# Moving twenty half-tile sums from GpSimd to VectorE in a fused retention and feed-forward kernel

## The chip, the cores and the metric

The kernel runs on one core of a Trainium2 chip. The metric is the device time of one execution in microseconds (us). A core has five instruction queues that run side by side and meet only at semaphores: TensorE (PE in the profile; its weight loads are listed as PEld), VectorE (DVE), ScalarE (ACT), GpSimd (POOL) and SyncE (SP, which here issues nearly all DMAs). Each queue runs its instructions in the order in which they were written; an instruction that waits holds back all that stand behind it.

## The reference

Inputs are q, k and v of shape 8 x 8 x 576 x 64 (batch, head, position, head width) and two weight matrices. First comes a decayed linear attention, then a feed-forward layer whose activation is h cos(h):

```python
scores = scale * np.matmul(q, k.transpose(0, 1, 3, 2))
Dmat = np.where(rel >= 0, gamma[:, None, None] ** rel[None, :, :], 0.0)
attn = np.matmul(scores * Dmat[None], v)          # 8 x 8 x 576 x 64
x = attn.transpose(0, 2, 1, 3).reshape(4608, 512)
h = x @ w_in                                      # 4608 x 2048
out = (h * np.cos(h)) @ w_out                     # 4608 x 512
```

## The kernel before, in words

**Stages.** The 4608 tokens are worked on as nine tiles of 512 (numbered j = 0 to 8; TB, NTB). The attention runs in chunks of 64 tokens with a carried state and fills a ring of transposed inputs (XT). One attention step of two chunks (`step`) is a short group of small matmuls: the inter-chunk part (L617), the state update (L638), the intra-chunk part (L627) and the scores of the next step (L608). ScalarE and VectorE empty its banks.

**First product.** `mlp1` multiplies a tile with w_in. Four matmuls of 512 columns (L844) make one 128 x 512 piece in a PSUM bank; ScalarE takes its cosine (L852, a sine with a shifted phase, into one of three CB buffers), and VectorE multiplies the two (L855) into the tile G. There are sixteen pieces, f = 0 to 15, for each 512 tokens. Tiles alternate between two G buffers.

**Second product.** For tile 0 it is done directly (`mlp2`, L869). For tiles 1 to 8 it is a seven-product scheme on 2 x 2 blocks (`strassen` and `product`, L963). G is cut into two halves of the inner dimension (f = 0 to 7 and 8 to 15) and two halves of the tokens; w_out is cut likewise. Products m3 and m4 use blocks of G as they are. Products m2 and m5 need S5, the sum of the two halves of the inner dimension. Product m1 needs S1, the sum of the two diagonal blocks. Products m6 and m7 need differences, which are written over two blocks of G. Each product has two halves of 128 tokens (t = 0, 1), of eight matmuls of 256 columns each. S5 and S1 exist once, so the sums of a tile wait until the products of the tile before have read them.

**The sums.** `token_sums(j, u)` writes three VectorE or GpSimd instructions for a quarter u = 0 to 3 of tile j: S5 (L923, 128 x 1024), S1 (L928, 128 x 512) and the differences in place (L932, 128 x 1024). They read and write SBUF in bf16. In the profile's groups both S5 and S1 appear as `s`; the line and the width tell them apart. A quarter u needs pieces 2u, 2u+1, 2u+8 and 2u+9 of the tile, so the last quarter needs the last piece. The constant POOLED = 4 decides the engine of L928: for tiles 1 to 3 it is VectorE, for tiles 4 to 8 GpSimd. L923 and L932 are always on VectorE.

**Recombination.** ScalarE saves or copies finished banks (`save` L1002, `plain` L1007), VectorE and GpSimd add and subtract (`add`, L998): VectorE's steps read a bank, GpSimd's combine what lies in SBUF. For the last tile the products are asked for in the order m3, m4, m1, m2, m5, m7, m6, and m6 is emptied in two halves (`tail`), each with a store of its own.

**What sets the order.** All operations are added to a program with a cost, the buffers that they read and write, and two marks. `arrange` then plays through the program with these costs: every engine takes, in a small window of its list, the first operation that is ready, but an operation marked `lazy` only if no other is ready. Operations marked `port` queue for one shared lock between VectorE and GpSimd. The order that comes out is written down as each engine's queue, with semaphore waits. A changed cost or engine of one operation can so change the order on all engines after it.

Of the kernel before, what the change touches and what calls it, by code (L numbers as in the profile page):

```python
# [240 lines left out]


SOLO = 8
POOLED = 4
STB = 0


# [51 lines left out]
def ap(t, size, p0, n, off, *dims):  # L299
    return bass.AP(t, p0 * size + off, [[size, n]] + [list(d) for d in dims])  # L300


class Kernel:
# [610 lines left out]
    def token_sums(self, j, u):  # L914
        gt, f = self.GT[j % 2], 2 * u

        def half(k, t):
            return ap(gt, NF * TB, 0, 128, (f + HF * k) * TB + HB * t, [TB, 2], [1, HB])

        def keys(k, *ts):  # L920
            return [("gt", j % 2, f + HF * k + i, x) for i in range(2) for t in ts for x in range(4 * t, 4 * t + 4)]

        self.P.add("dve", lambda e: e.tensor_tensor(  # L923
            ap(self.S5, HF * TB, 0, 128, f * TB, [1, 2 * TB]), ap(gt, NF * TB, 0, 128, f * TB, [1, 2 * TB]),
            ap(gt, NF * TB, 0, 128, (f + HF) * TB, [1, 2 * TB]), ALU.add),
            r=keys(0, 0, 1) + keys(1, 0, 1), w=[("s5", f), ("s5", f + 1)], cost=0.62, port=True, lazy=True)
        eng = "pool" if j >= POOLED else "dve"
        self.P.add(eng, lambda e: e.tensor_tensor(  # L928
            ap(self.S1, HF * HB, 0, 128, f * HB, [HB, 2], [1, HB]), half(0, 0), half(1, 1), ALU.add),
            r=keys(0, 0) + keys(1, 1), w=[("s1", f), ("s1", f + 1)], cost=1.04 if eng == "pool" else 0.36,  # L930
            port=True, lazy=eng == "dve")
        self.P.add("dve", lambda e: e.tensor_tensor(  # L932
            ap(gt, NF * TB, 0, 128, f * TB + HB, [HF * TB - HB, 2], [TB, 2], [1, HB]),
            ap(gt, NF * TB, 0, 128, f * TB + HB, [HF * TB, 2], [TB, 2], [1, HB]),
            ap(gt, NF * TB, 0, 128, f * TB, [HF * TB, 2], [TB, 2], [1, HB]), ALU.subtract),
            r=keys(0, 0, 1) + keys(1, 0, 1), w=keys(0, 1) + keys(1, 0), cost=0.62, port=True, lazy=True)
# [299 lines left out]
```

## Time and profile before

| | us |
|---|---|
| median of 6 runs (299.27 to 300.22) | 299.62 |
| the profiled execution | 299.28 |
| its span, first to last instruction | 297.6 |
| PE busy | 289.4 (97%) |
| DVE busy | 231.4 (78%) |
| ACT busy | 186.8 (63%) |
| POOL busy | 174.0 (58%) |
| L928 on POOL, 20 instructions | 28.3 |
| L928 on DVE, 12 instructions | 8.2 |

The span is what the profile shows; the 1.7 us between it and the execution's own time lie around it. A line of a group reads: source line, engine, operation, output and inputs by the program's names, shapes, count, then busy time and the mean duration of one in ns, then the idle time of the engine just before them with the instruction that ended it. A line of the timeline reads: start and duration in us, engine, line, operation, count, and in brackets the idle time before it. Neighbouring instructions of one kind are merged. The matmul rows are pipelined and overlap a little, so their starts are the better guide. The granted TensorE clock is 1.00 in every stretch of the profile but the last (0.99).

### The profile page before, as it was taken

How to read it: one execution, taken by the hardware profiler on the slowest of the kernel's cores; microseconds unless marked ns; L12 is line 12 of the kernel's file. 1: busy time of each engine (PE TensorE's matmuls, PEld its weight loads, DVE VectorE, ACT ScalarE, POOL GpSimd, SP SyncE). 2: the span in 40 equal slices, each digit the busy share in tenths (PEclk: the TensorE clock that was granted, in tenths of full speed). 3: DMA queues.
4: the chain of work that ended last, by engine and by line, in shares of the span. 5: the costliest groups of instructions: out<-in, count | busy, mean ns of one | idle time of the engine just before them, and what ended most of it. 6: DMA issues, size and time to landing. Idle time of an engine off the chain costs nothing.

```text
span 297.6 us, 8942 instructions
## 1 busy us (share of the span) xinstructions
PE 289.4 (97%) x3751; PEld 204.1 (69%) x3751; DVE 231.4 (78%) x369; ACT 186.8 (63%) x317; POOL 174.0 (58%) x166
## 2 busy tenths in 40 slices
PE   8998899999999999999999999999999999999996
PEld 2567568765788885777566766676677576666685
DVE  6785899999789389779957995899489738964961
ACT  6256767826588276676667667766776777555511
POOL 4566650979856487287508992899274017402923
PEclk9999999999999999999999999999999999999999
DMA  7999999999999999999789898998211011102024
GB/s 204 303 328 325 287 180 221 201 233 230 228 255 160 174 282 197 214 193 196 166 182 261 177 176 212 212 155 185 58 35 57 19 40 40 47 21 70 2 70 141
DMA packets 123895, 50.12 MB, mean 168 GB/s; under 512 B 82384, under 2 KB 123344, under 8 KB 123856
## 3 DMA queue, kind: packets, MB, share of 16 engines
q1 hardware_dynamic: 121744, 47.46, 72.5%
q0 software_dynamic: 2112, 2.10, 4.4%
q8 instruction: 29, 0.48, 0.7%
q14 instruction: 10, 0.08, 0.1%
HBM read 36.70 MB, written 9.44 MB: 155 GB/s over the span
## 4 chain that ended last, share of the span: by engine, by line
PE 84%; DVE 5%; SPq 4%; DMA 3%; ACT 2%; issue 1%; DVEq 0%
PE bk L844 38%; PE bk L963 32%; PE bk L869 5%; DMA gt<-in_moe_w_in_dram 3%; PE st L638 2%; SPq L433 2%; PE bk L617 2%; DVE gt L855 2%; SPq L466 1%; PE bk L608 1%; PE bk L627 1%; PE bk L565 1%; SPq L452 1%; DVE s L923 1%; PE bk L552 1%
## 5 line engine op out<-in xcount | busy, mean ns | idle before, releaser
L844 PE MATMUL bk<-xt,win 128*128 128x512 bf16 (+1 forms) x744 | 138.9, 331 | 2.7 <-DVE gt L855 0.7
L852 ACT ACTIVATE cb<-bk,cpi 128x512 bf16<-128x512 f32 x144 | 98.3, 688 | 54.8 <-PE bk L844 51.0
L855 DVE TENSOR_TENSOR gt<-bk,cb 128x512 bf16<-128x512 f32 x144 | 96.2, 684 | 42.2 <-ACT cb L852 37.0
L844 PEld LDWEIGHTS bk<-xt,win 128*128 128x128 bf16 x744 | 70.8, 98 | 43.6 <-DVE pt L712 1.1
L532 POOL TENSOR_TENSOR qnat<-qstg,wt 128x512 bf16<-128x512 f32 x34 | 40.9, 1221 | 20.6 <-DMA qstg<-in_q_dram 20.6
L998 POOL TENSOR_TENSOR sv<-sv,os 128x512 f32<-128x512 f32 x16 | 20.4, 1274 | 48.4 <-ACT os L1007 35.5
L680 ACT ACTIVATE sbd<-st 64x512 bf16<-64x512 f32 x58 | 34.3, 592 | 11.7 <-PE bk L608 10.4
L494 POOL CAST nat<-stg 128x512 bf16<-128x512 f32 x32 | 25.1, 791 | 20.0 <-DMA stg<-in_k_dram 15.5
L928 POOL TENSOR_TENSOR s<-gt 128x512 bf16<-128x512 bf16 x20 | 28.3, 1423 | 13.4 <-DVE gt L855 13.4
L932 DVE TENSOR_TENSOR gt<-gt 128x1024 bf16<-128x1024 bf16 x32 | 34.1, 1070 | 0.2
L522 POOL TENSOR_TENSOR nat<-stg,wt 128x512 bf16<-128x512 f32 x28 | 32.1, 1147 | 2.7 <-DMA stg<-in_v_dram 2.6
L963 PE MATMUL bk<-tw,gt 128*128 128x256 bf16 x256 | 32.1, 273 | 0.0
L923 DVE TENSOR_TENSOR s<-gt 128x1024 bf16<-128x1024 bf16 x32 | 29.5, 931 | 3.1 <-PE bk L963 2.8
L963 PE MATMUL bk<-wout,s 128*128 128x256 bf16 x256 | 31.6, 273 | 0.1
L963 PE MATMUL bk<-wout,gt 128*128 128x256 bf16 x256 | 30.8, 273 | 0.0
L680 ACT ACTIVATE xt<-bk 128x256 bf16<-128x256 f32 (+1 forms) x64 | 26.9, 488 | 4.5 <-PE bk L869 2.0
L963 PEld LDWEIGHTS bk<-wout,s 128*128 128x128 bf16 x256 | 24.5, 98 | 6.3 <-DVE s L923 0.5
L963 PEld LDWEIGHTS bk<-tw,gt 128*128 128x128 bf16 x256 | 24.2, 98 | 6.0 <-ACT sv L1002 0.6
L963 PEld LDWEIGHTS bk<-wout,gt 128*128 128x128 bf16 x256 | 24.8, 98 | 4.4
L653 DVE TENSOR_TENSOR pt<-bk,tri 128x256 bf16<-128x256 f32 (+3 forms) x39 | 20.4, 543 | 1.6 <-PE bk L608 1.3
L1007 ACT ACTIVATE os<-bk 128x512 f32<-128x512 f32 x16 | 9.6, 597 | 11.9 <-PE bk L963 11.8
L998 POOL TENSOR_TENSOR sv<-sv 128x512 f32<-128x512 f32 x8 | 12.9, 1609 | 6.7 <-ACT sv L1002 6.3
(76 smaller groups left out, 277.0 us busy)
## 6 DMA issues: line engine op xcount, KB each, us to landing
out_dram<-os SPq DMA_DIRECT2D x31, 256.0 KB, 3.1
qstg<-in_q_dram SPq DMA_DIRECT2D x12, 512.0 KB, 5.5
stg<-in_k_dram SPq DMA_DIRECT2D x24, 256.0 KB, 4.3
stg<-in_v_dram SPq DMA_DIRECT2D x24, 256.0 KB, 5.6
stg<-in_k_dram SPq DMA_DIRECT2D x4, 512.0 KB, 7.6
stg<-in_v_dram SPq DMA_DIRECT2D x4, 512.0 KB, 7.3
gt<-in_moe_w_in_dram SPq DMA_DIRECT2D x4, 512.0 KB, 8.5
wout<-in_moe_w_out_dram POOLq DMA_DIRECT2D x4, 512.0 KB, 11.9
```

What stands on the lines that cost most here:

```text
L494: self.P.add(eng, lambda e: e.tensor_copy(dst, src), r=r, w=w, cost=cost, port=eng == "pool" or half == 0.75)
L522: self.P.add(eng, lambda e: e.tensor_tensor(ap(self.NAT[na], 2 * DM, 0, 128, DM, [D, H], [1, D]), ap(self.STG[st], 2 * DM, 0, 128, DM, [D, ...
L532: self.P.add(eng, lambda e, x=x: e.tensor_tensor(ap(self.QNAT[slot], 2 * DM, 0, 128, x * DM, [D, H], [1, D]), ap(self.QSTG[slot], 2 * DM, ...
L680: self.P.add(eng, (lambda e: e.activation(*io(), AF.Copy)) if eng == "act" else (lambda e: e.tensor_copy(*io())), r=r, w=w, cost=0.175 + 0 ...
L844: inst = e.matmul(self.bk(box.i, 0, 128, i * n, n), ap(self.WIN, 4 * DFF, 0, 128, c * DFF + 128 * f, [1, 128]), ap(self.XT, 4 * XR, 0, 128 ...
L852: self.P.add("act", lambda e: e.activation(ap(cb, TB, 0, 128, 0, [1, m]), self.bk(box.i, 0, 128, 0, m), AF.Sin, bias=self.CPI.ap(), scale= ...
L855: self.P.add("dve", lambda e: e.tensor_tensor(ap(gt, NF * TB, 0, 128, f0 * TB + lo - TB * j, [TB, len(fs)], [1, n]), self.half_bank(box.i, ...
L923: self.P.add("dve", lambda e: e.tensor_tensor(ap(self.S5, HF * TB, 0, 128, f * TB, [1, 2 * TB]), ap(gt, NF * TB, 0, 128, f * TB, [1, 2 * TB]),
L928: self.P.add(eng, lambda e: e.tensor_tensor(ap(self.S1, HF * HB, 0, 128, f * HB, [HB, 2], [1, HB]), half(0, 0), half(1, 1), ALU.add), r=ke ...
L932: self.P.add("dve", lambda e: e.tensor_tensor(ap(gt, NF * TB, 0, 128, f * TB + HB, [HF * TB - HB, 2], [TB, 2], [1, HB]), ap(gt, NF * TB, 0 ...
L963: inst = e.matmul(self.bk(box.i, 0, 128, at * HB, HB), ap(lt, lsize, 0, 128, loff + f * lstep + 128 * t, [1, 128]), ap(rt, rsize, 0, 128, ...
L998: self.P.add(eng, lambda e: e.tensor_tensor(out(), a(), b(), op), r=r, w=w, cost=1.2 if eng == "pool" else 0.09 + 0.00104 * n * HB, port=e ...
```

## The change

The S1 sum is always put on VectorE, for all tiles, with the cost and the `lazy` mark that it had there for tiles 1 to 3. The constant POOLED goes. Twenty instructions (tiles 4 to 8, four each) change their engine, and the arithmetic stays the same.

```diff
-POOLED = 4
 ...
-        eng = "pool" if j >= POOLED else "dve"
-        self.P.add(eng, lambda e: e.tensor_tensor(
+        self.P.add("dve", lambda e: e.tensor_tensor(
             ap(self.S1, HF * HB, 0, 128, f * HB, [HB, 2], [1, HB]), half(0, 0), half(1, 1), ALU.add),
-            r=keys(0, 0) + keys(1, 1), w=[("s1", f), ("s1", f + 1)], cost=1.04 if eng == "pool" else 0.36,
-            port=True, lazy=eng == "dve")
+            r=keys(0, 0) + keys(1, 1), w=[("s1", f), ("s1", f + 1)], cost=0.36, port=True, lazy=True)
```

The planner writes other queues for it from the first sums of tile 4 on (after 159.36 us of the profile before); up to there all queues are the same. What is moved:

- VectorE: L928 stands a little after L923 of its quarter, and L932 of that quarter after it. Up to a few L855, the mask of an attention step (L653) or an L998 trade places with the sums.
- GpSimd: the twenty L928 are gone. Some casts and L998 trade places.
- TensorE, tiles 4 and 5: m2 and m5 stand later, behind further L844 and behind the attention step that followed them. Single halves of m4 and m7 pass an attention step.
- TensorE, last tile: in place of m1 m1 m2 m2 m5 m5 (two halves each) the order is m5, m2, m1, m1, m2, m5. Before them stand m3 and m4, after them m7 and m6, as before.
- VectorE, end: the order of the last three L998 is first half of m6, m7, second half of m6, where it was m7, first half, second half. The three last stores on SP follow suit: L984, L979, L984 in place of L979, L984, L984.
- SP and ACT: some stores pass a load of q or v, one pair of transposing DMAs (L574, L580) is swapped, and some evictions (L1007) pass one to three L852.

## The prediction

> **What bounds the kernel now.** I read the busy table first, then the busy time by stage, then TensorE's waits behind the point where the queues begin to differ (148 us on), then the groups of the three sums, and last the timeline of the end.
>
> ```profile
> span 297.6 us, 8942 instructions
> PE 289.4 (97%) x3751; PEld 204.1 (69%) x3751; DVE 231.4 (78%) x369; ACT 186.8 (63%) x317; POOL 174.0 (58%) x166
> ```
> ```profile
> 60.00:90.00 30.00, 29.99 (x493) 21.37 (x491) 26.82 (x43) 18.64 (x34) 23.92 (x24) 1.00 1.12 236
> ...
> 150.00:180.00 30.00, 30.00 (x404) 20.34 (x403) 23.83 (x33) 21.05 (x37) 23.48 (x21) 1.00 0.95 200
> 180.00:210.00 30.00, 30.00 (x385) 20.63 (x384) 23.96 (x34) 20.61 (x37) 22.48 (x20) 1.00 0.89 185
> 210.00:240.00 30.00, 30.00 (x403) 20.24 (x401) 22.45 (x33) 21.61 (x39) 9.79 (x7) 1.00 0.12 38
> ```
> ```profile
> PEld bk L617 <- issue: 0.8, 2, 0.4
> PEld bk L963 <- ACT sv L1002: 0.6, 2, 0.3
> PEld bk L963 <- DVE s L923: 0.5, 1, 0.5
> ```
>
> The columns of the stages are the stretch and its length, then busy time of PE, PEld, DVE, ACT and POOL. The reader is to see that TensorE has no gap in the stage where the twenty sums lie: 30.00 of 30.00 us, three times. From 148 us to the end its weight loads wait 1.9 us in all, and none of that is for a sum on GpSimd. Four L844 take 0.86 us and eight L963 take 0.87 us wherever they stand in the chain. So the stage is TensorE's, and the change neither adds nor drops a matmul. It can gain in it at most the two waits of 0.4 us marked issue; it can lose whatever it makes TensorE wait.
>
> ```profile
> L928 POOL TENSOR_TENSOR s<-gt 128x512 bf16<-128x512 bf16 x20 | 28.3, 1423 | 13.4 <-DVE gt L855 13.4
> ...
> L932 DVE TENSOR_TENSOR gt<-gt 128x1024 bf16<-128x1024 bf16 x21 | 22.0, 1052 | 0.2
> L923 DVE TENSOR_TENSOR s<-gt 128x1024 bf16<-128x1024 bf16 x21 | 20.1, 967 | 0.3
> ```
>
> These are the groups from 148 us on. Clear of GpSimd, L923 and L932 take 0.68 us each (0.60 from start to start); here they average 0.97 and 1.05, because they stand beside GpSimd work.
>
> ```profile
> 278.27 1.27 POOL L998 TENSOR_TENSOR sv<-sv,os 128x512 f32<-128x512 f32 x1
> ...
> 279.49 3.83 POOL L928 TENSOR_TENSOR s<-gt 128x512 bf16<-128x512 bf16 x3
> 280.75 1.56 DVE L923 TENSOR_TENSOR s<-gt 128x1024 bf16<-128x1024 bf16 x1
> 282.24 1.30 DVE L998 TENSOR_TENSOR os<-bk,sv 128x512 f32<-128x512 f32 x2
> ...
> 284.05 1.28 DVE L923 TENSOR_TENSOR s<-gt 128x1024 bf16<-128x1024 bf16 x2
> ...
> 286.14 1.91 PE L963 MATMUL bk<-tw,s 128*128 128x256 bf16 x16
> ...
> 288.76 1.26 POOL L998 TENSOR_TENSOR sv<-sv 128x512 f32<-128x512 f32 x1 [5.43 <-ACT sv L1002]
> ...
> 294.75 1.13 SPq L984 DMA_DIRECT2D out_dram<-os  x2
> 295.07 0.42 DVE L998 TENSOR_TENSOR os<-bk,sv 128x256 f32<-128x256 f32 x1 [0.44 <-PE bk L963]
> ```
>
> The end is where the two halves of the question meet. GpSimd finishes the last S1 at 283.3 us; VectorE the last S5 at 285.3 us; TensorE comes free of m4 at 286.1 us and starts m1 at once. VectorE is thus 0.8 us ahead of TensorE, and GpSimd carries a quarter of its sums.
>
> **The change part by part.** The sum is made against the profiled execution: 299.28 us, span 297.6, which is 0.34 below the median of the six.
>
> *Twenty L928 leave GpSimd.* They are 28.3 us of its time, and 13.4 us of waiting before them. GpSimd is on no wait of TensorE behind 148 us, so on the path this is 0. The casts behind them come earlier; whatever waited for those is 0 as well. L923 and L932 get back toward 0.68: at most 21 x (0.29 + 0.37) = 13.8 us of VectorE's time, part of it only, as casts and L998 still stand in the way. Cover of this zero: TensorE is full, so VectorE's time is spare in the middle.
>
> *Twenty L928 join VectorE.* Clear ones last 0.41 us and take 0.33 from start to start (147.93 to 148.26); the twelve of tiles 1 to 3 average 0.68 with a longest of 1.49 (beside an L998 of GpSimd). So 20 x 0.33 = 6.6 us at the least and 20 x 1.49 = 29.8 us at the most; from the mean, 13.6. Sixteen or seventeen of them lie in the 130 us in which VectorE is busy 22 to 24 us out of 30: there they fit into idle time. Three lie in the last 16 us, taken up below.
>
> *The new order in the middle (tiles 4 to 7).* The moved halves and attention steps cost TensorE nothing in themselves: in the chain an attention step takes 0.85 us of TensorE, whether L844 or L963 stands beside it. Price of new waits: the S5 of the last quarter of tiles 4 and 5 now comes after six to seven L855, just ahead of m2 and m5, which stand right behind an attention step. If it is late, TensorE waits there with all its queue, the next L844 among it, and ScalarE after that. Lower bound 0, as behind 148 us today. Upper bound from the stage that already runs this way: tiles 1 to 3 have all sums on VectorE, with GpSimd as busy (23.92 of 30), and there L923 let the weight loads wait twice, 0.8 and 0.5 us, in three tiles; at that rate four tiles would wait 1.7 us. I take 0, since the stage from 60 to 90 us, with the same mix, still has PE at 29.99, and keep 1.7 for the range. SP's stores that pass a load, the swapped transposes (needed some steps later), and the evictions that pass up to three L852 are put at 0 by the same cover; if it fails they are part of the 1.7.
>
> *The end.* L855 of the last piece ends in both kernels with TensorE's last L844, so VectorE is free at 280.75. From there, start to start, the new queue is L932 0.60, L998 0.61, L923 0.60, L928 0.33, L998 0.62, L932 0.60, L923 0.60, L928 0.33, L932 0.60: 4.89 us. The last L923 starts at 285.64 and ends at 286.32. GpSimd has nothing in that time (its L998 end by 279.5, the next comes at 288.76), so the collision that made an L923 take 1.56 is gone, and is gone from this sum. m5 may start some 0.06 us after L923 (as at 148.06 after 148.00): 286.38, where TensorE started m1 at 286.14. The first eight matmuls after a wait take 0.98 in place of 0.87. TensorE is late by 0.24 + 0.11 = 0.35 us. Behind it are ten half products back to back. Their other needs are met: m2 waits for VectorE's L998 (to 286.9; m5's half runs to 287.4), m1 for the last L928 (287.3; m2's half runs to 288.2), m7 for the last L932 (287.9).
>
> The copies then come as m1, m2, m5, the last at 292.4; GpSimd's three L998 run back to back from 290.8, as ScalarE saves m1 1.7 us + 0.35 later, and end at 294.6, where the last ended at 293.5. VectorE does the first half of m6 at 294.5 and m7 after it, to 295.55; the second half of m6 ends at 295.9, not 295.49. The store of m7 (256 KB) is issued at 295.6 in place of 294.3, and the last one (128 KB) behind it at 295.97, not 295.53: 0.44 late. It now has 256 KB just ahead of it. In the profile the three stores move 512 KB in one go, at 325 to 347 GB/s, and land 2.2, 2.1 and 1.7 us after issue. If the last shares freely, it lands 0.44 later than before; if it goes strictly behind m7's store, that lands at 297.8 and this one at 297.8 + 0.38 = 298.2 against 297.23, 0.95 later. I take 0.8, nearer to the second, since the transfers already ran without a gap.
>
> Sum: 0 + 0 + 0 + 0.8 = 0.8 us. 299.28 becomes 300.1; on the median 299.62 becomes 300.4.
>
> A rule weighed: the Trainium skill (GPSIMD Engine Reference, 4.1 Engine selection) says to put elementwise work on VectorE, as GpSimd takes about twice as long with two inputs. The rows agree on the instruction (1.16 us clear on GpSimd, 0.41 on VectorE), and by the rule the change would save 20 x 0.75 = 15 us of engine time and come out no slower. The sum goes by which engine TensorE waits for at the end, and there it is the quicker engine that has no slack.
>
> **The rivals.** *The sums are hidden at the end too.* If VectorE gains some tenths (say L932 of the first quarter fits between the L855, which pace with ScalarE at 0.86 against 0.60 for VectorE), S5 is ready at 286.0, TensorE does not wait, and only the reversed stores remain, 0.1 to 0.3 us: 299.7 to 299.9. For it: the missing slack is only 0.24 us. Against: the queue is in order and L932 stands behind all six L855. *TensorE waits in the middle as well.* One to three waits at tiles 4 and 5, of 0.5 to 0.8 each as at tiles 1 to 3: 0.8 + 0.5 to 0.8 + 1.7, so 300.9 to 302.1. For it: the last S5 comes just in time there, and GpSimd still casts at 22 to 23 of 30. Against: sums on VectorE no longer collide with L928. *Faster.* The two issue waits of TensorE (0.8 us together) hang on how the queues fall, and may vanish with the new order; together with an end that does not wait this gives 298.9 to 299.0. It decides only if both happen: either alone leaves the time within 0.6 us of before. No other gain is to be had, TensorE being full.
>
> **How the numbers follow.** Late end alone (my forecast) 0.46; also in the middle 0.24; hidden 0.22; faster 0.08. What a measurement of this kernel can tell from no change is about 0.2%, 0.6 us: 300.2 and 299.0. The late end spans 299.62 + (0.35 + 0.1) to + (0.35 + 0.95), 300.1 to 300.9, so that about a quarter of it (0.10) is within 0.2%; its own range is that. Slower: 0.36 + 0.24 = 0.60; same: 0.22 + 0.10 = 0.32; faster: 0.08. The range from 299.7 to 301.8 leaves out the faster case, a part of the hidden one and the worst of the middle.
>
> **What would show it.** L928 on VectorE x32, none on GpSimd; means of L923 and L932 behind 148 us down by 0.1 to 0.3; PE still 30.00 of 30 in the stages from 150 to 270, or else waits on L923 or L928 at tiles 4 and 5; at about 286 us a wait of PE's weight load for L923; TensorE's and VectorE's last instructions some 0.35 to 0.4 us later than before, counted from the last L844; and the last store issued close behind an L979. I am wrong if TensorE runs through at 286, if the waits of the middle exceed 1.7 us, or if the planner's costs are so far off that masks (L653) come late.

## The result, and the profile after

The changed kernel takes 301.88 us (median of 21 runs, 300.87 to 302.69), the kernel before beside it 299.73 us (47 runs). The ratio is 1.006, with a 95% interval from 1.0047 to 1.0074: the change makes the kernel slower by 0.6%, about 1.8 us, where 0.8 was forecast. (The two medians lie 2.15 us apart, a little more than this ratio.) The profiled execution took 301.25 us, its span is 299.5.

The busy table of the changed kernel:

```profile
PE 290.1 (97%) x3751; PEld 203.9 (68%) x3751; DVE 232.0 (77%) x392; ACT 187.2 (62%) x317; POOL 143.4 (48%) x146
```

GpSimd is freed of 30.6 us. VectorE has taken over twenty sums (three more rows are attention masks that are written in two pieces instead of one) and is busy only 0.6 us longer than before (231.4). The groups of the sums from 148 us on (line, engine, tiles, shapes, count, busy time, mean in ns):

```profile
L929 DVE TENSOR_TENSOR gt<-gt 128x1024 bf16<-128x1024 bf16 x21 | 15.9, 757 | 0.0
L922 DVE TENSOR_TENSOR s<-gt 128x1024 bf16<-128x1024 bf16 x21 | 15.5, 739 | 0.2
L926 DVE TENSOR_TENSOR s<-gt 128x512 bf16<-128x512 bf16 x21 | 13.7, 652 | 0.0
```

The lines of the changed file stand two or three lower: L922 is S5 (L923 before), L926 is S1 (L928), L929 the differences (L932), L843, L851, L854 the first product (L844, L852, L855), L960 the second (L963). S5 went from 967 to 739 ns and the differences from 1052 to 757. What S1's leaving GpSimd has to do with that, and what the new order, is taken up in the last section.

The stages (stretch, length, busy time of PE, PEld, DVE, ACT, POOL), and TensorE's weight loads' waits from 148 us on:

```profile
150.00:180.00 30.00, 29.93 (x397) 19.50 (x395) 23.34 (x35) 21.39 (x37) 17.32 (x17) 1.00 0.99 201
180.00:210.00 30.00, 29.78 (x379) 19.87 (x377) 22.68 (x38) 20.91 (x37) 16.25 (x16) 1.00 0.84 187
210.00:240.00 30.00, 30.00 (x411) 21.03 (x410) 24.11 (x42) 20.58 (x36) 4.38 (x3) 1.00 0.11 37
```
```profile
PEld bk L960 <- DVE s L922: 1.1, 2, 0.8
PEld bk L960 <- DVE gt L854: 0.8, 2, 0.4
PEld bk L616 <- issue: 0.8, 2, 0.4
PEld bk L843 <- issue: 0.5, 1, 0.5
PEld bk L843 <- ACT cb L851: 0.5, 1, 0.5
PEld bk L616 <- ACT cb L851: 0.4, 1, 0.4
PEld bk L960 <- ACT sv L999: 0.3, 1, 0.3
```

The first two stages are no longer full, and the waits have grown from 1.9 to 4.4 us. Busy time hides most of that: an L843 row lasts 0.38 us while the next one starts 0.22 us after it, so two starts can move apart by 0.16 us before a gap shows. The waits in turn overstate it: the weight load that waits 0.53 us at 178.15 moves the matmul's start by only 0.23 (0.45 behind the one ahead in place of 0.22). A better measure is the start of an attention step (L617, L616 after) and of the fourth one behind it, a stretch that holds one tile's work:

| from one attention step to the fourth behind it | before | after |
|---|---|---|
| the stretch with tile 4's sums (167.16 to 196.45; 167.57 to 197.21) | 29.29 | 29.64 |
| with tile 5's (to 225.75; to 227.09) | 29.30 | 29.88 |
| with tile 6's (to 255.27; to 256.50) | 29.52 | 29.41 |
| from there to the first half of tile 7's m7 (279.15; 280.39) | 23.88 | 23.89 |
| from there to the end of the span (297.56; 299.53 in the traces) | 18.41 | 19.14 |

The five rows add up to 1.56 us: 0.82 in the middle and 0.73 at the end. (With the spans rounded to 297.6 and 299.5 the end comes to 18.45 and 19.11, as some expectations below have it.) The remaining 0.41 of the 1.97 us between the two spans lies before 167 us, where the queues of both kernels are the same up to 159. There m2 of tile 3 waits 0.75 us for S5 at 148.5 in this execution, 0.55 in the profile before, and between 0.41 and 0.71 in the nine experiments whose queues are also the same up to there; and an attention step waits 0.38 at 145.4, which two of the nine also show and the profile before does not. I put this part down to the execution and not to the change.

The end in the timeline of the changed kernel:

```profile
281.99 0.68 DVE L929 TENSOR_TENSOR gt<-gt 128x1024 bf16<-128x1024 bf16 x1
...
286.86 0.68 DVE L922 TENSOR_TENSOR s<-gt 128x1024 bf16<-128x1024 bf16 x1
...
287.59 0.44 PEld L960 LDWEIGHTS bk<-wout,s 128*128 128x128 bf16 x5 [0.34 <-DVE s L922]
...
291.98 1.27 POOL L995 TENSOR_TENSOR sv<-sv 128x512 f32<-128x512 f32 x1 [12.70 <-ACT sv L999]
293.32 2.49 POOL L995 TENSOR_TENSOR sv<-sv,os 128x512 f32<-128x512 f32 x2
...
295.67 1.35 DVE L995 TENSOR_TENSOR os<-bk,sv 128x256 f32<-128x256 f32 x3 [6.47 <-PE bk L960]
...
296.72 0.37 SPq L976 DMA_DIRECT2D out_dram<-os  x1
297.13 0.47 SPq L981 DMA_DIRECT2D out_dram<-os  x1
```

The walk of VectorE from L929 to the last L922 takes 4.87 us (286.86 less 281.99), as forecast: 4.89 to the start of the last S5. TensorE then waits for that S5 and starts m5 7.21 us behind the stretch's beginning, where m1 started at 6.99. GpSimd's three last subtractions and additions run back to back; m7's store (L976) and the last one (L981) are issued close together at the very end.

### The profile page after: what moved, and what is told of

Its sections match the earlier page's. It is cut to its first block, busy times and chain, and to the rows that moved or that the text cites. A ratio compares the mean times of both kernels' runs of the same rounds, so it can differ in the third digit from the quotient of the medians.

```text
span 299.5 us, 8949 instructions
## 1 busy us (share of the span) xinstructions
PE 290.1 (97%) x3751; PEld 203.9 (68%) x3751; DVE 232.0 (77%) x392; ACT 187.2 (62%) x317; POOL 143.4 (48%) x146
## 4 chain that ended last, share of the span: by engine, by line
PE 79%; DVE 7%; SPq 4%; ACT 4%; DMA 3%; issue 1%; DVEq 0%
PE bk L843 37%; PE bk L960 29%; PE bk L868 5%; DMA gt<-in_moe_w_in_dram 3%; DVE gt L854 2%; PE st L637 2%; SPq L432 2%; PE bk L616 2%; SPq L465 1%; PE bk L607 1%; ACT cb L851 1%; DVE s L922 1%; PE bk L626 1%; ACT sbd L679 1%; PE bk L564 1%
## 5 line engine op out<-in xcount | busy, mean ns | idle before, releaser
L843 PE MATMUL bk<-xt,win 128*128 128x512 bf16 (+1 forms) x744 | 138.6, 331 | 3.1 <-ACT xt L679 0.8
L851 ACT ACTIVATE cb<-bk,cpi 128x512 bf16<-128x512 f32 x144 | 98.3, 688 | 52.3 <-PE bk L843 48.5
L854 DVE TENSOR_TENSOR gt<-bk,cb 128x512 bf16<-128x512 f32 x144 | 96.5, 684 | 43.2 <-ACT cb L851 37.8
L843 PEld LDWEIGHTS bk<-xt,win 128*128 128x128 bf16 x744 | 70.4, 98 | 45.1 <-issue 1.6
L531 POOL TENSOR_TENSOR qnat<-qstg,wt 128x512 bf16<-128x512 f32 x34 | 38.9, 1163 | 20.7 <-DMA qstg<-in_q_dram 14.3
L679 ACT ACTIVATE sbd<-st 64x512 bf16<-64x512 f32 x58 | 34.3, 592 | 12.9 <-PE bk L607 11.3
L493 POOL CAST nat<-stg 128x512 bf16<-128x512 f32 x32 | 22.5, 709 | 30.9 <-DMA stg<-in_k_dram 26.6
L521 POOL TENSOR_TENSOR nat<-stg,wt 128x512 bf16<-128x512 f32 x28 | 32.9, 1175 | 4.0 <-DMA stg<-in_v_dram 3.7
L960 PE MATMUL bk<-tw,gt 128*128 128x256 bf16 x256 | 32.1, 273 | 0.0
L960 PE MATMUL bk<-wout,s 128*128 128x256 bf16 x256 | 30.8, 273 | 0.3 <-DVE s L922 0.3
L960 PE MATMUL bk<-wout,gt 128*128 128x256 bf16 x256 | 31.1, 273 | 0.0
L679 ACT ACTIVATE xt<-bk 128x256 bf16<-128x256 f32 (+1 forms) x64 | 27.0, 487 | 3.8 <-DVE pt L652 3.2
L960 PEld LDWEIGHTS bk<-tw,gt 128*128 128x128 bf16 x256 | 24.3, 98 | 6.4 <-DVE gt L854 0.8
L960 PEld LDWEIGHTS bk<-wout,s 128*128 128x128 bf16 x256 | 24.5, 98 | 5.9 <-DVE s L922 1.1
L960 PEld LDWEIGHTS bk<-wout,gt 128*128 128x128 bf16 x256 | 24.9, 98 | 5.0
L922 DVE TENSOR_TENSOR s<-gt 128x1024 bf16<-128x1024 bf16 x32 | 24.9, 781 | 3.0 <-PE bk L960 2.8
L929 DVE TENSOR_TENSOR gt<-gt 128x1024 bf16<-128x1024 bf16 x32 | 26.9, 842 | 0.0
L926 DVE TENSOR_TENSOR s<-gt 128x512 bf16<-128x512 bf16 x32 | 21.5, 672 | 0.0
L999 ACT ACTIVATE sv<-bk 128x512 f32<-128x512 f32 x16 | 9.6, 597 | 13.1 <-PE bk L960 13.1
```

What stands on the lines that cost most here:

```text
L493: self.P.add(eng, lambda e: e.tensor_copy(dst, src), r=r, w=w, cost=cost, port=eng == "pool" or half == 0.75)
L521: self.P.add(eng, lambda e: e.tensor_tensor(ap(self.NAT[na], 2 * DM, 0, 128, DM, [D, H], [1, D]), ap(self.STG[st], 2 * DM, 0, 128, DM, [D, ...
L531: self.P.add(eng, lambda e, x=x: e.tensor_tensor(ap(self.QNAT[slot], 2 * DM, 0, 128, x * DM, [D, H], [1, D]), ap(self.QSTG[slot], 2 * DM, ...
L679: self.P.add(eng, (lambda e: e.activation(*io(), AF.Copy)) if eng == "act" else (lambda e: e.tensor_copy(*io())), r=r, w=w, cost=0.175 + 0 ...
L843: inst = e.matmul(self.bk(box.i, 0, 128, i * n, n), ap(self.WIN, 4 * DFF, 0, 128, c * DFF + 128 * f, [1, 128]), ap(self.XT, 4 * XR, 0, 128 ...
L851: self.P.add("act", lambda e: e.activation(ap(cb, TB, 0, 128, 0, [1, m]), self.bk(box.i, 0, 128, 0, m), AF.Sin, bias=self.CPI.ap(), scale= ...
```

## The experiments

Two theories of the middle went into the first runs. By the one (A) TensorE waits because the planner's new order of the queues is worse; by the other (B) because VectorE now has more to do. Times are against runs of the kernel before on the same chip. "Stretches" are the first three rows of the table above; where an expectation counts attention steps, they run from the 24th to the 28th, the 32nd and the 36th.

**Splitting the change by tile.** First only tile 8 is moved, then all but tile 8 (tiles 4 to 7):

```diff
-        eng = "pool" if j >= POOLED else "dve"
+        eng = "pool" if POOLED <= j < 8 else "dve"
```

> Only the last tile's four S1 sums go to VectorE; tiles 4 to 7 keep theirs on GpSimd. All queues are as before up to the first sums of tile 8, and TensorE's tail has the new order. If the end costs what the two profiles show (18.45 us from the last L844's end to the end of the span before, 19.11 after), the time is 0.6 to 0.8 us above before (300.2 to 300.4 against 299.6), with m5 of the last tile waiting for the last L923. Rival, the end is hidden and all the loss is in the middle: within 0.2 us of before.

```diff
-POOLED = 4
+POOLED = 8
```

> Tiles 4 to 7 have S1 on VectorE with the new order of the middle, tile 8 keeps it on GpSimd and the old end. If the middle costs what the profiles show (0.4 us at tile 4 and 0.5 to 0.6 at tile 5), the time is 0.8 to 1.2 us above before. If those waits were the chance of one execution, it is within 0.3 us.

Tile 8 alone: 300.53 against 299.59 us, ratio 1.0027 [1.0008, 1.0046]. The three stretches of the middle are as before (29.29, 29.31, 29.51), the end takes 19.15 us, as in the full change (19.14). Tiles 4 to 7 alone: 300.90 us, 1.0034 [1.0014, 1.0054], with stretches of 29.64, 29.88 and 29.42, again as in the full change. The two halves are separate, and 0.27% and 0.34% add up to the whole 0.6%.

**Order or work.** In one kernel the planner is told the old engines, so that all queues keep their old order, and L928 is put on VectorE afterwards, where GpSimd's would have stood. The other is its opposite: the changed kernel's order, with L928 of tiles 4 to 8 given back to GpSimd.

```diff
+        for op in self.ops:
+            op.eng = op.late or op.eng
         self.settle()
 ...
+        op.late = "dve"                          # old order, sums on VectorE
+        op.late = "pool" if j >= 4 else None     # new order, sums on GpSimd
```

> The planner is given the old engines and costs, so that the order of TensorE, ScalarE and SyncE is that of before; only when the queues are written are all L928 put on VectorE, at the places in time where GpSimd had them. Theory A, the loss of the middle comes from TensorE's new order (L844 in dense runs behind an attention step, whose banks are emptied late): no wait at tiles 4 and 5, 0 to 0.3 us above before; and as m1 with its early S1 stands first at the end, no wait there either. Theory B, it comes from VectorE's added work itself: 0.8 us or more above before, with TensorE waiting on L855 or masks.

> The planner is given the new engines and costs, so that TensorE, ScalarE and SyncE have the new order; when the queues are written the L928 of tiles 4 to 8 go back to GpSimd. Theory A (order): 0.9 us for the middle and some 0.3 for the reversed stores at the end, 1.2 us above before, with the waits of TensorE at tiles 4 and 5 still there. Theory B (VectorE's work): 0 to 0.4 us above before.

The old order with the sums on VectorE takes 305.23 us, 1.0191 [1.0164, 1.0218], far more than theory A gave (0 to 0.3 us); B had said 0.8 us or more. The stretches are 31.54, 29.81 and 30.24. The timeline of this kernel around tile 4 (L930 is S1, L935 the differences, L857 the product with the cosine, L619 the attention step, L846 the first product):

```profile
165.06 1.25 DVE L925 TENSOR_TENSOR s<-gt 128x1024 bf16<-128x1024 bf16 x1
166.23 1.26 DVE L930 TENSOR_TENSOR s<-gt 128x512 bf16<-128x512 bf16 x1
167.42 0.68 DVE L857 TENSOR_TENSOR gt<-bk,cb 128x512 bf16<-128x512 f32 x1
168.02 1.50 DVE L935 TENSOR_TENSOR gt<-gt 128x1024 bf16<-128x1024 bf16 x1
...
165.72 1.49 POOL L524 TENSOR_TENSOR nat<-stg,wt 128x512 bf16<-128x512 f32 x1
...
168.15 0.41 PE L619 MATMUL bk<-qt,sbd 128*128 128x64 bf16 x8 [0.67 <-DVE gt L857]
```

An S1 that lasts 0.41 clear takes 1.26 beside a cast of GpSimd, L857 comes late behind it, and TensorE waits for L857. So the added work does hurt where it stands in the way (B), and with the planner's new order the 5.7 us come down to 1.8.

The new order with the sums on GpSimd takes 301.45 us, 1.0054 [1.0039, 1.0068]; the stretches are 30.26, 29.88 and 29.41. The waits of L843 and L616 (0.5, 0.5, 0.4) are there unchanged although VectorE has none of the moved work, and tile 5 loses the same 0.58 us. (Tile 4 loses more than in the change, since here an S5 takes 1.56 us beside GpSimd's L928 and TensorE waits 0.66 us for it at 181.72.) What the change costs in the middle is thus the price of the order (A).

**Which wait in the order.** In the changed kernel's timeline, at tile 4:

```profile
175.47 1.21 ACT L679 ACTIVATE sbd<-st 64x512 bf16<-64x512 f32 x2 [0.95 <-PE bk L607]
176.70 0.69 ACT L851 ACTIVATE cb<-bk,cpi 128x512 bf16<-128x512 f32 x1
...
177.49 0.69 DVE L854 TENSOR_TENSOR gt<-bk,cb 128x512 bf16<-128x512 f32 x1 [0.34 <-ACT cb L851]
...
178.15 2.29 PEld L843 LDWEIGHTS bk<-xt,win 128*128 128x128 bf16 x12 [0.53 <-issue]
180.79 0.30 PEld L616 LDWEIGHTS bk<-qt,sbd 128*128 128x128 bf16 x8 [0.36 <-ACT cb L851]
```

The profile names no releaser for L843 ("issue"), but its first matmul starts at 178.18, just as L854 ends and its bank is empty; L854 waited for the cosine L851, and that stood behind ScalarE's two copies of the attention state (L679). In the new order m2 and m5 are pushed behind, so that soon behind an attention step come sixteen (tile 4) and twenty-four (tile 5) L843 in a row, without L960 between them. They need a bank every 0.86 us while the two state copies hold ScalarE for 1.2. Before, the same copies ran at 175.93 to 177.14, and behind the first eight L844 there stood sixteen L963:

```profile
177.54 1.91 PE L963 MATMUL bk<-wout,s 128*128 128x256 bf16 x16
```

This is theory C. To test it, the changed kernel keeps its order and leaves out ScalarE's state copies after step 25 and half the columns of those after step 29, so that the later steps read an older state:

```diff
+        u0, m = (1, 1) if g == 29 else (u0, m)
         for hp, eng in enumerate(engs):
+            op = self.move(...)
+            op.skip = g == 25
```

> The changed kernel with its order kept, but ScalarE's two state copies after attention step 25 (tile 4) are left out and those after step 29 (tile 5) copy one of the two batches only; the later attention steps then read an older state, so this part of the computation is not done. Theory C, TensorE waits at tiles 4 and 5 for a bank, since the cosine (L851) and with it L854 stand behind ScalarE's two state copies (1.21 us) and the new order gives no L960 in between: the waits of TensorE's L843 there (0.53 and 0.47) go to 0.1 or less, the time is 0.6 to 0.9 us below the changed kernel, 0.9 to 1.2 above before. Theory D, VectorE's own queue (sums ahead of L854) holds the bank: no change, 1.8 above before.

300.81 us, 1.0032 [1.0014, 1.0050], with stretches of 29.41, 29.59 and 29.41. The first two lose 0.23 and 0.29 us. Of the 0.93 that these two stretches had cost, 0.52 is shown to hang on ScalarE's state copies. The other 0.41 is not traced to a cause: in the stretch of tile 5, where only half of the columns were left out, part of the wait remained, as did the two waits of 0.4 for L854. The waits of this kernel (L846 and L854 are L843 and L851 of the change):

```profile
PEld bk L846 <- issue: 0.2, 1, 0.2
PEld bk L846 <- ACT cb L854: 0.2, 1, 0.2
```

They were 0.5 each; the expectation had 0.1 or less.

**The end.** The two kernels above speak of the end too. In the old order, with all S1 on VectorE, m1 starts 6.99 us behind the stretch's beginning, GpSimd's last L998 ends at 14.37 and the span at 18.41: as before, to the hundredth. In the new order, with S1 on GpSimd, the end takes 19.28 us. So the end, too, is the price of the order and not of the work that VectorE took over. Which piece of the order it is, the next kernels ask.

With tile 8's sums on VectorE I left out the second and third S1 of that tile, so that VectorE is ahead again:

```diff
+        op.skip = j == 8 and u in (1, 2)
```

> As tile8 (only the last tile's S1 on VectorE), but the second and third of its four L928 are left out when the queues are written, so that half of S1 of the last tile is old data. VectorE reaches the last L923 some 0.66 us earlier, all other order is that of tile8. If m5's wait for that L923 and the reversed stores share the 0.8 us of tile8 as predicted (0.35 and 0.45), TensorE's wait at the end goes and 0.4 to 0.5 us above before remain. If the wait is all of it: 0 to 0.2 us. If the stores are all of it: 0.8 us as in tile8.

300.62 us, 1.0027 [1.0004, 1.0050]. m5 starts 6.98 us behind the stretch's beginning, without a wait for S5, but the second product then waits 0.19 us for VectorE's L998, which still comes late; the end takes 18.99 us instead of 19.15. TensorE's wait for S5 is therefore not what the end costs. My next suspect was the reversed pair of stores, so one kernel puts m7's subtraction and store back in front of the first half of m6:

```diff
+        for x, y in (("m6", "m7"), ("m6 store", "m7 store")):
+            self.ops.remove(ends[x])
+            self.ops.insert(self.ops.index(ends[y]) + 1, ends[x])
         self.settle()
```

> Tile 8's S1 on VectorE as in the first run, but the two last pairs put back to the order of before: VectorE does m7's L998 ahead of the first half of m6, and SP issues m7's 256 KB store ahead of the first 128 KB one. Everything else as in the first run, whose profile was 0.66 longer behind the last L844 than before and whose time was 0.3% above. If the reversed stores make most of that (my theory now), the stretch behind the last L844 is 0.2 to 0.3 longer than before, TensorE's delay alone, and the time 0.1% above. If TensorE's delay or something on VectorE makes it, the stretch stays 0.6 to 0.7 longer and the time 0.2 to 0.3% above.

301.19 against 300.08 us, 1.0048 [1.0026, 1.0070], and the end takes 19.45 us: longer, not shorter. That suspect falls. The timeline of this kernel (L1002 is L998):

```profile
291.00 1.27 POOL L1002 TENSOR_TENSOR sv<-sv 128x512 f32<-128x512 f32 x1 [12.70 <-ACT sv L1006]
292.35 2.49 POOL L1002 TENSOR_TENSOR sv<-sv,os 128x512 f32<-128x512 f32 x2
...
294.93 1.35 DVE L1002 TENSOR_TENSOR os<-bk,sv 128x512 f32<-128x512 f32 x3 [6.70 <-PE bk L967]
```

m7's L1002 starts 0.09 us after GpSimd's last one ends (292.35 + 2.49 = 294.84); in the profile before it was 293.61 after 293.52. GpSimd's chain ends 15.43 us behind the stretch's beginning, before at 14.37. The delay fits the new order of the products (m5, m2, m1, m1, m2, m5), in which m1, m2 and m5 all finish in the last three of these six halves and GpSimd's three operations pile up; with the first half of m6 ahead of m7 the end is 0.30 us shorter than without. To test that, I took one of the three off GpSimd:

```diff
-            add("pool", lambda: sv[2], lambda: sv[2], lambda: sv[0], ALU.add, ...)
+            add("dve" if last else "pool", lambda: sv[2], lambda: sv[2], lambda: sv[0], ALU.add, ...)
```

> Tile 8's S1 on VectorE as in the first run, and the last tile's L998 of m1 (the first of GpSimd's three at the end) on VectorE, which has 6.5 us of idle time there; the planner then by itself does m7's L998 and store first, as before. My theory now: TensorE's new product order brings m1 to an end two products later, GpSimd's three L998 of 1.25 us each run back to back after it and end 1.06 later against the last L844 than before, and m7's L998 and its store wait for them; the reversal only softened this, which is why undoing it made the stretch longer (19.49 against 19.11 and 18.45). With one of the three gone the stretch behind the last L844 is 18.6 to 18.8 and the time 0.1% above before. If the stores or TensorE's delay are the cause, it stays at 19.0 to 19.2 and 0.25 to 0.3%.

300.34 against 299.77 us, 1.0024 [1.0004, 1.0045]; the end takes 19.04 us, 0.11 less than with tile 8 alone and short of the 0.3 to 0.5 that I expected. The pieces of the end, counted from the stretch's beginning:

| | before | tile 8 alone | two S1 left out | m7 first | m1's L998 on VectorE |
|---|---|---|---|---|---|
| first product behind m4 starts | 6.99 | 7.21 | 6.98 | 7.21 | 7.21 |
| GpSimd's last L998 ends | 14.37 | 15.43 | 15.27 | 15.43 | 15.02 |
| VectorE's last L998 ends | 16.34 | 16.63 | 16.48 | 16.87 | 16.57 |
| m7's store (256 KB) is issued | 15.18 | 16.34 | 16.18 | 16.24 | 15.83 |
| m7's store lands | 17.36 | 18.55 | 18.40 | 18.43 | 18.02 |
| stores of 128 KB behind it | 2 | 1 | 1 | 2 | 2 |
| last store lands | 18.11 | 18.86 | 18.70 | 19.16 | 18.75 |
| span ends | 18.41 | 19.15 | 18.99 | 19.45 | 19.04 |

In the last column VectorE's end is late by 0.23 us, just what TensorE is late by, while the span is late by 0.63. The rows of the stores say where the rest lies. In all five kernels m7's store lands about 2.2 us after its issue, each store behind it lands 0.3 to 0.4 us after the one ahead, and the span ends 0.3 us after the last landing. So the end goes by when m7's store is issued and by how many stores follow it. Before, with m7 first and with m1's L998 on VectorE, where two follow, 2.9 us pass from that issue to the last landing; the issue is late by 1.06 and 0.65 us and the span by 1.04 and 0.63, and so is GpSimd's last L998 (1.06 and 0.65), for which m7 waits. In tile 8 alone m7's store is late by 1.16, but only one store follows it, which gives 0.4 back. That is why a piece less on GpSimd gained only 0.11: the planner then put m7 ahead of both halves of m6 again. The path of the end is thus the new order of the products, GpSimd's three operations, m7, its store and the stores that queue behind it. TensorE's delay of 0.22 is a part of GpSimd's 1.06, and the reversal is not a cost.

**Which tiles cost.** If the sums belong on GpSimd, more of them there should not hurt. POOLED was lowered to 3 and to 1 (all tiles):

> One step the other way: tile 3's S1 go to GpSimd as well (POOLED = 3). If a tile's S1 on VectorE costs TensorE some tenths wherever GpSimd has room, it is 0.3 to 0.8 us below before (tile 3 has the wait of 0.5 us of m2 for L923 in the profile before). If GpSimd, which there has casts for 17 of 30 us, only moves the collision, it is within 0.3 us of before.

> All S1 on GpSimd (POOLED = 1). If only VectorE's load counts: 0.5 to 1.5 us below before. If GpSimd's casts, 20 to 24 of 30 us busy at tiles 1 and 2, become late and with them attention steps: 0 to 2 us above before.

299.15 and 299.25 against 299.63 us: 0.9979 [0.9958, 1.0000] and 0.9981 [0.9962, 0.9999], a touch faster than the kernel before at most, as both intervals reach to 1 or next to it. In their traces m2 of tile 3 no longer waits for S5 near 148 us. Then the choice was made tile by tile, from the stretches:

```diff
-        eng = "pool" if j >= POOLED else "dve"
+        eng = "pool" if j in (4, 5, 8) else "dve"       # and, as another kernel: j in (3, 4, 5, 8)
```

> S1 on GpSimd for tiles 4, 5 and 8, on VectorE for 1, 2, 3, 6 and 7: the kernel before with tiles 6 and 7 moved as in the change. If the cost of the change lies at tiles 4, 5 and 8 alone, this is 0 to 0.1% below before, with attention steps from the twenty-eighth to the thirty-second as before and the end as before. If moving any tile costs, it is 0.1 to 0.3% above.

> S1 on GpSimd for tiles 3, 4, 5 and 8, on VectorE for 1, 2, 6 and 7. From the segments of the profiles: GpSimd at tile 3 was worth 0.1 to 0.5 us, tiles 4 and 5 on GpSimd avoid 0.9, tile 8 avoids 0.7, and tile 6 on VectorE was 0.1 us shorter. If these add up by tile, 298.9 to 299.3, about as with GpSimd from tile 3 on, no more than 0.2 better. If each order is a draw of its own by the planner, anything from 299 to 301.

With tiles 6 and 7 on VectorE and the rest as before: 299.79 against 299.77 us, 0.9996 [0.9978, 1.0014], stretches 29.29, 29.30, 29.41, and an end of 18.40 us. Moving tiles 6 and 7 costs nothing that shows; the cost lies at tiles 4, 5 and 8. With tile 3 on GpSimd as well: 298.72 against 300.08 us, 0.9958 [0.9943, 0.9974], faster than both kernels. Its profile, though, has the same span as the one with tiles 4, 5 and 8 (297.0 us both, 297.6 before), and the two stood against different runs of the kernel before. That it is faster is shown, that it is faster by as much as 0.4% rests on six runs.

## Why the prediction was right and where it was wrong

The direction was right, the size too small, and the cause half right. The ratio of 1.006, put on the 299.62 us of the first runs, is 301.4 us (301.0 to 301.8 by its interval): inside the range of 299.7 to 301.8, at its upper end, and 1.0 above the likeliest case. That the range held is in part luck: its upper end had room for 1.7 us of waits in the middle, but for S5, and another wait came.

*GpSimd's relief is worth nothing to TensorE, VectorE's time in the middle is spare.* Right: 30.6 us less on GpSimd gained no time, VectorE's busy time grew by 0.6 us, and the means of S5 and the differences fell by 0.23 and 0.30 us, as foreseen (0.1 to 0.3). The rule that was weighed (the Trainium skill, GPSIMD Engine Reference, 4.1 Engine selection: elementwise work on VectorE) holds for the instruction and not for the kernel: with all S1 on GpSimd the kernel is as fast as before or 0.2% faster, with all on VectorE 0.6% slower.

*The new order in the middle: "I take 0".* This step failed. It measures 0.82 us in the profile and 0.3% (about 1.0 us) as a run of its own. I had looked at what each moved piece costs TensorE, and at one new wait (S5 ahead of m2 and m5). That wait is not what came. The rows that would have told are ScalarE's: two state copies of 0.6 us each behind an attention step, and a cosine every 0.86 us. Moving m2 and m5 behind left a dense row of first-product matmuls just there, which need a cosine per 0.86 us for their banks. The rival "TensorE waits in the middle as well" had the place (tiles 4 and 5) and the size (0.5 to 1.7 us) right, and the mechanism wrong. The zero also rested on PE at 29.99 of 30 us from 60 to 90 us. The next two stages before, with all sums on VectorE as well, show 29.64 (90 to 120) and 29.94 (120 to 150), and busy time is a poor witness anyway: the stages with a loss of 0.35 and 0.58 us still show 29.93 and 29.78.

*The end: TensorE late by 0.35, the stores by 0.45.* The walk of VectorE came out to 0.02 us and the wait where it was foretold; TensorE was late by 0.22. The 0.11 for slower matmuls behind a wait was a misreading: no run shows it, and eight matmuls behind the wait at 148.06 before and behind that at 287.60 after take 0.88, against 0.87 elsewhere. The sum of 0.8 measured 0.73 in the profile and 0.27% (0.8 us) as a run of its own. The stores' part came out right in size (0.45 forecast, 0.51 measured) and half right in its reason. That the last store goes strictly behind m7's is so: it lands 0.3 us after it. But I blamed the reversal for it; what makes m7 late is the end of GpSimd's three operations, which the prediction had (294.6 in place of 293.5) without seeing that m7 hangs on it.

*Faster, by the loss of the two issue waits.* They are still there, 0.8 us in all.

The likeliest case reached to 300.9 at most; the second rival, with a chance of 0.24, gave 300.9 to 302.1. In size it is what happened, by another wait than it named.

## What to carry to other kernels

Whether an operation belongs on the quick engine or the slow one is decided by whom the bounding engine waits for, and in a kernel whose order is planned from costs one engine's change redraws the queues of all: check the new order's dense rows against the engine that must empty their banks. Compare starts of the same piece of work in two traces, since busy time of a pipelined engine hid waits of some tenths here. Where a late chain is suspected, follow every consumer of its last result: a planner's odd-looking order may be the remedy and not the harm.

## What the runs showed of the hardware that was not expected

The same twenty sums on VectorE cost 0.6% or 1.9%, by the order of the queues alone. Beside GpSimd's two-input operations a 0.41 us sum took 1.26 and a 0.68 us difference 1.50 (rows of the old order with the sums on VectorE). The sum ended 0.28 us after the operation of GpSimd beside it (167.49 after 167.21), the difference 0.54 (169.51 after 168.97), somewhat less than each takes when clear: they seem to have done their work once GpSimd was done. GpSimd is slowed too: its L524 takes 1.04 us at 170.38 in that timeline, where no sum runs, and 1.49 beside VectorE's sums. The Trainium skill (SBUF — State Buffer, Summary: rules for kernel authors) says that when VectorE has two inputs in SBUF and GpSimd's operation reads SBUF, the second one to start is held until the first has finished; these rows agree.

That VectorE is busy for only 0.6 us more is not the work of S1's leaving GpSimd alone. At one and the same order the twenty sums cost it 5.6 us (231.4 to 237.0, old order) or 5.2 (226.8 to 232.0, new order); the new order by itself gives about as much back. The move brings S5's mean down (to 743 ns with the old order kept), while the differences fall by the order (788 ns with the new order and S1 still on GpSimd, 945 with the old order and S1 on VectorE).
